# Later, split additions of exponentials, six conversion buffers, two tiles for the turned q and k, and another order at the outset and at the first norm, in an attention kernel followed by a SwiGLU FFN

## The chip, the cores and the metric

The kernel runs on one core of a Trainium2 chip. The metric is the device time of one execution in microseconds (us). Executions of one kernel agree to about 0.3%. A ratio is the mean time of one kernel's fast runs over the mean of the other's of the same rounds, so it is not quite the ratio of the medians that are quoted beside it. "Same" means within 2%.

## The reference

```python
# q, k, v: (8, 12, 448, 64) float32; g_q, g_k: (64,); w_gate, w_val: (768, 1536), w_out: (1536, 768), float64
q_n, k_n = rmsnorm(q, g_q), rmsnorm(k, g_k)            # over the 64 of each head
scores = q_n @ k_n.T / sqrt(64)
attn = exp(scores - max); attn = attn / (attn.sum(-1) + 1e-9)
x = (attn @ v), heads side by side                      # (3584, 768)
xn = x / sqrt(mean(x*x) + 1e-6) * rms_g
out = (silu(xn @ w_gate) * (xn @ w_val)) @ w_out        # (3584, 768) float32
```

There are 8 sequences with 6 pairs of heads each, so 48 pairs, numbered on through the sequences. A sequence has 448 rows: three blocks of 128 and a last one of 64, which the kernel calls "rests".

## The kernel before

The engines run in an order fixed by hand. Each `pe(fn)` is one step of TensorE (PE); `after(n, fn)` puts work for other engines n steps later in the program. The attention of later pairs is mixed with the FFN of earlier sequences. During the first 300 us the float64 weights are also turned into float32 with integer operations, in 72 pieces:

```python
NW, NH = 27, 14                                   # slots for weights
raw_pool, cv_pool = pool("c_raw", 6), pool("c_cv", 4)
...
def split(raw):                                   # ACT; raw is the loaded float64
    top = cv_pool.tile([128, BW], I32, name="top")
    nc.scalar.activation(top.bitcast(F32), hi.bitcast(F32), ACT.Abs)                   # L719
    nc.scalar.activation(lo, lo.bitcast(U32), ACT.Copy, scale=2.0**-29)                # L720
def join(lo, hi, top):                            # DVE: three instructions, L725 to L727
...
def convert():                                    # one turn, called about once per PE step
    n = turn_of["n"]
    ...
    if 0 <= n - 4 < len(pieces):                  # POOL: L763, frees top and raw
        nc.gpsimd.tensor_tensor(data(key).bitcast(I32), top, lo, ALU.add)
    if 0 <= n - 3 < len(pieces):
        st["cv", n - 3] = join(*st.pop(("cv", n - 3)))
    if 0 <= n - 2 < len(pieces):
        st["cv", n - 2] = split(st.pop(("raw", n - 2)))
    if n < len(pieces):
        st["raw", n] = load_raw(pieces[n][1])     # transfer, 384 KB, into one of six raw buffers
    if 0 <= n - 6 < len(pieces):
        keep(pieces[n - 6][0])
```

A `raw` buffer lives from its transfer to the addition in POOL (GpSimd), because `lo` and `hi` are views of it. Six raw buffers thus mean: the transfer of piece n waits for the addition of piece n-6.

The sums of exponentials, for pairs past the first seven, on POOL:

```python
def add():                                        # in score()
    rest = st["e", g, "rest"]
    for j in range(2):
        r = across(j)
        es = st["es", g, j] = tmp.tile([128, S], F32, name="es", tag="es", bufs=4)
        nc.gpsimd.tensor_tensor(es, st["e", g, 0, j], st["e", g, 1, j], ALU.add)
        nc.gpsimd.tensor_tensor(es, es, st["e", g, 2, j], ALU.add)
        nc.gpsimd.tensor_tensor(es[r], es[r], rest[r], ALU.add)
if NK - 1 in cs and not direct(g):
    after(4 if g == NPAIR + 1 else 1, add)
```

The rests of the next sequence are loaded in the third pair of a sequence and normed, on POOL, in the fourth and fifth. For sequence 2 these are pairs 9 and 10, while weights are still being converted:

```python
def rms():                                        # in norm_rests(), POOL
    nc.gpsimd.tensor_scalar(ms, ms, 1.0 / D, 1e-6, ALU.mult, ALU.add)
    nc.gpsimd.tensor_tensor(rq, ms[0:D], half[0:D], ALU.pow)
    nc.gpsimd.tensor_tensor(rest[0:D], rest[0:D], rq..., ALU.mult)
    for place in range(2):
        nc.gpsimd.tensor_tensor(st["rr", b][own(place), lo:hi], ms[own(1), :, place], half[own(1), :, place], ALU.pow)
...
def some_rests(g):
    b, hp = divmod(g, NPAIR)
    if g == 1:
        norm_rests(0, 3, NPAIR)
    elif hp in (3, 4):
        norm_rests(b + 1, 3 * (hp - 3), 3 * (hp - 2))
...
        if hp == 2:
            load_rests(b + 1, nc.sync)
            load_v_rests(b + 1)
```

The order at the first norm of x (pair 7), and the copies of the turned (transposed) q and k out of PSUM, where PE's results land:

```python
        if g == NPAIR + 1:
            pe(lambda: rms_x(0))
            pe(lambda: score(g, (1, 2)))
            pe(lambda: norm_x(0))
        pe(lambda: sums(g - 1))
...
    nc.scalar.activation(dst[:, 0, :], ps[:, 0:S], ACT.Copy, scale=gqk[:, 0:1])    # L519, q by ACT
    nc.vector.tensor_copy(dst[:, 1, LAST], ps[:, S:])                              # L520, k's last columns by DVE
```

## Time and profile before

| | before |
|---|---|
| median of 4 runs (lowest, highest) | 1641.48 us (1638.43, 1642.02) |
| span of the profiled execution | 1636.1 us |
| PE busy in that span | 1595.4 us (98%) |
| PE idle before 480 us / from 480 to 1400 us | 32 us / 1.3 us |

The time is PE's time. So the profile is read by looking for the places where PE stands still or runs at half clock (its granted clock falls to 0.5), and for what it waits for there. All of them lie before 480 us. The lines are in the prediction below. In the tables by stage the columns are: stretch and its length, then busy time and number of instructions of PE, of PE's weight loads, of DVE (VectorE), ACT (ScalarE) and POOL, then the granted clock of PE, the DMA share and GB/s.

### The profile page before, as it was taken

To read this page: it belongs to the slowest core of one execution; us is meant where nothing else is said; L and a number is where in the kernel's file an instruction comes from. 1 tells how busy PE (TensorE), PEld (TensorE's weight loads), DVE (VectorE), ACT (ScalarE), POOL (GpSimd) and SP (SyncE) were. 2 spreads that over 40 slices of the span, in tenths; PEclk is the share of its full clock that TensorE was granted. 3 is DMA by queue.
4 is the path that set the end of the run, shared out by engine and by line. 5 is a ranking of instruction groups with operands and counts; after the bars stand their busy time and mean duration, and the time that the engine had idled before them with its cause. 6 is when DMAs were issued, how large, how long until landed. Compare 5 with 4: busy or idle time off the path is not lost.

```text
span 1636.1 us, 21612 instructions
## 1 busy us (share of the span) xinstructions
PE 1595.4 (98%) x7328; PEld 1125.6 (69%) x7328; DVE 873.6 (53%) x1490; ACT 476.4 (29%) x944; POOL 672.0 (41%) x706
## 2 busy tenths in 40 slices
PE   7999899999999999999999999999999999999998
PEld 3344444577865787758885588847877587969974
DVE  4779888568872354525564245633556234433431
ACT  6755444322232223222322223222232123100110
POOL 7867786545434433433542354324534322200000
PEclk8999999999999999999999999999999999999999
DMA  7657456456665654485554655466544564557641
GB/s 188 195 163 223 156 178 197 154 190 227 226 216 154 202 156 135 124 260 148 160 151 138 175 159 155 140 189 202 160 137 118 161 179 116 150 183 237 174 143 49
DMA packets 264587, 276.81 MB, mean 169 GB/s; under 512 B 79124, under 2 KB 261396, under 8 KB 264468
## 3 DMA queue, kind: packets, MB, share of 16 engines
q1 hardware_dynamic: 262740, 274.95, 56.3%
q8 instruction: 60, 0.98, 0.3%
q10 hardware_dynamic: 1600, 0.39, 0.1%
q14 instruction: 59, 0.48, 0.1%
q0 software_dynamic: 128, 0.00, 0.0%
HBM read 235.93 MB, written 39.32 MB: 168 GB/s over the span
## 4 chain that ended last, share of the span: by engine, by line
PE 83%; DVE 9%; POOL 3%; DMA 2%; issue 1%; ACT 1%; SPq 0%; DVEq 0%; POOLq 0%; ACTq 0%
PE ff L878 38%; PE ff L1076 21%; PE av L579 6%; PE sc L532 6%; PE ff L973 3%; PE den L592 2%; PE sc L556 2%; PE ff L1107 2%; DVE rd L600 2%; PE tr L515 1%; DVE top L725 1%; DVE top L726 1%; DVE top L727 1%; DVE w L835 1%; POOL rs L495 1%
## 5 line engine op out<-in xcount | busy, mean ns | idle before, releaser
L878 PE MATMUL ff<-x,w 128*128 128x224 f32 x1770 | 360.9, 355 | 3.6 <-ACT p L911 1.9
L878 PEld LDWEIGHTS ff<-x,w 128*128 128x128 f32 x1770 | 333.5, 191 | 13.5 <-issue 6.5
L543 POOL TENSOR_TENSOR es<-e 128x448 f32<-128x448 f32 x82 | 94.0, 1146 | 543.5 <-ACT e L536 540.2
L878 PE MATMUL ff<-xs,w 128*128 128x224 f32 x1326 | 272.2, 354 | 1.9 <-DVE u L890 1.6
L878 PEld LDWEIGHTS ff<-xs,w 128*128 128x128 f32 x1326 | 248.6, 190 | 8.1 <-issue 5.2
L1076 PE MATMUL ff<-w,h 128*128 128x384 f32 x600 | 203.4, 488 | 0.0
L600 DVE RECIPROCAL rd<-rd 128x448 f32<-128x448 f32 x41 | 121.1, 2953 | 128.4 <-ACT rd L599 128.4
L536 ACT ACTIVATE e<-sc,rs 128x448 f32<-128x448 f32 x288 | 162.0, 633 | 42.4 <-PE sc L532 40.8
L1076 PEld LDWEIGHTS ff<-w,h 128*128 128x128 f32 x600 | 112.6, 190 | 78.3 <-issue 4.6
L532 PE MATMUL sc<-qkT 64*128 64x448 f32 x576 | 140.8, 583 | 7.5 <-ACT e L572 6.0
L579 PE MATMUL av<-e,vt 128*64 128x448 f32 x576 | 119.0, 548 | 0.0
L1076 PE MATMUL ff<-w,so 128*128 128x384 f32 x338 | 116.6, 488 | 2.0 <-DVE y L1037 2.0
L532 PEld LDWEIGHTS sc<-qkT 64*128 64x128 f32 x576 | 54.6, 189 | 90.5 <-issue 68.7
L495 POOL TENSOR_TENSOR rs<-ms,mhalf 128x12 f32<-128x12 f32 (+1 forms) x50 | 113.2, 2263 | 4.2
L1107 PE MATMUL ff<-x,w 128*128 128x448 f32 x288 | 114.5, 552 | 0.0
L890 DVE TENSOR_TENSOR cc<-ff,u 128x448 f32<-128x448 f32 x84 | 52.3, 623 | 88.7 <-PE ff L878 88.6
L544 POOL TENSOR_TENSOR es<-es,e 128x448 f32<-128x448 f32 x82 | 94.4, 1152 | 7.8 <-ACT e L536 1.5
L545 POOL TENSOR_TENSOR es<-es,e 64x448 f32<-64x448 f32 x82 | 94.6, 1154 | 6.4
L1076 PEld LDWEIGHTS ff<-w,so 128*128 128x128 f32 x338 | 63.3, 190 | 46.4 <-DVE y L1037 3.9
L1107 PEld LDWEIGHTS ff<-x,w 128*128 128x128 f32 x288 | 54.5, 194 | 52.9 <-issue 51.3
L579 PEld LDWEIGHTS av<-e,vt 128*64 128x64 f32 x576 | 37.2, 137 | 76.9 <-issue 73.4
L763 POOL TENSOR_TENSOR w<-top,raw 128x384 int32<-128x384 int32 x72 | 76.1, 1073 | 21.8 <-DVE top L727 6.3
(123 smaller groups left out, 1964.4 us busy)
## 6 DMA issues: line engine op xcount, KB each, us to landing
w<-kept SPq DMA_DIRECT2D x480, 192.0 KB, 3.1
w<-kept_o SPq DMA_DIRECT2D x290, 192.0 KB, 2.6
kept<-w SPq DMA_DIRECT2D x94, 192.0 KB, 3.7
top<-kept SPq DMA_DIRECT2D x72, 192.0 KB, 2.8
qk<-in_q_dram SPq DMA_DIRECT2D x48, 192.0 KB, 3.9
qk<-in_k_dram SPq DMA_DIRECT2D x96, 96.0 KB, 3.1
vt<-in_v_dram SPq DMA_DIRECT2D x48, 192.0 KB, 2.5
raw<-in_moe_w_gate_dram SPq DMA_DIRECT2D x24, 384.0 KB, 4.3
```

The costliest lines, as they stand in the source:

```text
L495: nc.gpsimd.tensor_tensor(st["rs", g][:, cols], ms, mhalf[:, cols], ALU.pow)
L532: nc.tensor.matmul(ps[:, 0:S], lhsT=qkT[r, 1, c * 128:(c + 1) * 128], rhs=qkT[r, 0, :], start=True, stop=True)
L536: nc.scalar.activation(e, ps[:, 0:S], ACT.Exp, scale=rs[:, n:n + 1])
L543: nc.gpsimd.tensor_tensor(es, st["e", g, 0, j], st["e", g, 1, j], ALU.add)
L544: nc.gpsimd.tensor_tensor(es, es, st["e", g, 2, j], ALU.add)
L545: nc.gpsimd.tensor_tensor(es[r], es[r], rest[r], ALU.add)
L579: nc.tensor.matmul(av[own(j), 0:S], lhsT=vt[:, j, c], rhs=st["e", g, c, j], start=False, stop=(c == NK - 1), skip_group_check=True)
L600: nc.vector.reciprocal(rd, rd)
L763: nc.gpsimd.tensor_tensor(data(key).bitcast(I32), top, lo, ALU.add)
L878: nc.tensor.matmul(bank[:, w * HT:(w + 1) * HT], lhsT=wt[:, c * 128:(c + 1) * 128], rhs=x[:, c, :], start=onto is None and w == c == 0, st ...
L1076: nc.tensor.matmul(ps, lhsT=a, rhs=data(("wo", b, name, c)), start=first and c == 0, stop=c == NFP - 1, skip_group_check=True)
L1107: nc.tensor.matmul(bank[w][:, 0:S], lhsT=data(key)[:, c * 128:(c + 1) * 128], rhs=st["x", 0, half][:, c, :], start=half == c == 0, stop=ha ...
```

## The change

Its intent is to take away the stops in the first 300 us: POOL's additions of exponentials are to leave gaps for the conversion, and the conversion is to run further ahead. It has five parts, which this document calls A to E.

A, the additions come later and in three parts:

```diff
-        def add():
-            rest = st["e", g, "rest"]
+        def first():
             for j in range(2):
-                r = across(j)
                 es = st["es", g, j] = tmp.tile([128, S], F32, name="es", tag="es", bufs=4)
                 nc.gpsimd.tensor_tensor(es, st["e", g, 0, j], st["e", g, 1, j], ALU.add)
-                nc.gpsimd.tensor_tensor(es, es, st["e", g, 2, j], ALU.add)
-                nc.gpsimd.tensor_tensor(es[r], es[r], rest[r], ALU.add)
+        def more(of):
+            for j in range(2):
+                r = across(j) if of == "rest" else slice(0, 128)
+                e = st["e", g, of] if of == "rest" else st["e", g, of, j]
+                es = st["es", g, j]
+                nc.gpsimd.tensor_tensor(es[r], es[r], e[r], ALU.add)
         if NK - 1 in cs and not direct(g):
-            after(4 if g == NPAIR + 1 else 1, add)
+            n = 3 if g == NPAIR + 1 else 2
+            after(n, first)
+            after(n + 2, lambda: more(2))
+            after(n + 3, lambda: more("rest"))
```

B, six conversion buffers, and two slots fewer for weights:

```diff
-    NW, NH = 27, 14
+    NW, NH = 25, 14
-    raw_pool, cv_pool = pool("c_raw", 6), pool("c_cv", 4)
+    raw_pool, cv_pool = pool("c_raw", 6), pool("c_cv", 6)
```

C, two tiles for the turned q and k (the users of the tile follow, not shown):

```diff
-            st["qkT", g] = qkT_pool.tile([128, 2, S], F32, name="qkT")
+            for part in ("qT", "kT"):
+                st[part, g] = qkT_pool.tile([128, S], F32, name=part)
```

D, the outset (cut; the second half of the rests' norm, `rms_k`, also comes one step later there, and the two multiplications that change with it, of the mean and of the gains, cost the same number of instructions):

```diff
-    load_rests(0, nc.scalar)
+    load_rests(0, 0, nc.scalar)
+    load_rests(0, 1, nc.sync)
     load_pair(1)
...
     squares(0, 0)
-    norm_rests(0, 0, 1)
     warm(9)
     pe(idle)
+    norm_rests(0, 0, 1)
...
-    squares(2, 0)
...
+            pe(lambda: score(0, (0,)))
             pe(lambda: rests(0))
+            pe(lambda: score(0, (1, 2)))
+            squares(2, 0)
             squares(2, 1)
-            pe(lambda: score(0, (0, 1, 2)))
```

E, the first norm of x after the sums:

```diff
+            pe(lambda: score(g, (1,)))
             pe(lambda: rms_x(0))
-            pe(lambda: score(g, (1, 2)))
-            pe(lambda: norm_x(0))
+            pe(lambda: score(g, (2,)))
         pe(lambda: sums(g - 1))
         if g == NPAIR + 1:
+            pe(lambda: norm_x(0))
             begin(0, 15)
```

## The prediction

> **What bounds the kernel now.** I read the page first, then the busy time of each engine by stage, then what TensorE (PE) waited for, then the same waits for the other engines, then the order of time around the longest stops. The page says that PE is the bound, and the slices say where it is not:
>
> ```profile
> PE 1595.4 (98%) x7328; PEld 1125.6 (69%) x7328; DVE 873.6 (53%) x1490; ACT 476.4 (29%) x944; POOL 672.0 (41%) x706
> ...
> PE   7999899999999999999999999999999999999998
> ```
>
> The table by stage (length, then the busy time of PE, PE's weight loads, DVE, ACT, POOL, then the granted clock):
>
> ```profile
> 0.00:20.00 20.00, 13.02 (x50) 7.89 (x50) 4.76 (x13) 9.53 (x18) 14.99 (x31) 0.83 0.98 231
> 20.00:45.00 25.00, 23.23 (x114) 8.60 (x116) 17.10 (x32) 17.15 (x35) 19.65 (x23) 0.93 0.65 164
> 45.00:107.00 62.00, 56.83 (x289) 21.72 (x286) 46.39 (x76) 41.39 (x84) 49.23 (x51) 1.00 0.64 195
> 107.00:300.00 193.00, 181.49 (x622) 88.05 (x621) 173.00 (x236) 95.26 (x194) 140.85 (x133) 0.97 0.56 172
> 300.00:480.00 180.00, 173.39 (x846) 133.21 (x845) 131.32 (x227) 46.27 (x90) 78.62 (x83) 0.99 0.67 217
> 480.00:1400.00 920.00, 918.70 (x4417) 681.06 (x4416) 421.45 (x733) 247.66 (x482) 363.30 (x374) 1.00 0.55 160
> ```
>
> From 480 to 1400 us PE is idle for 1.3 us in all, so nothing that the change does there can be worth anything. What can be won lies before 480 us: 7.0 us idle in the first stage, 1.8 in the second, 5.2 in the third, 11.5 in the fourth (the weights are converted there, and DVE is 90% and POOL 73% busy), 6.6 in the fifth: 32 us. To that comes PE work at half clock: a mean of 0.97 over 193 us is 5.8 us more clock time taken away, some 3 us of work. So even a change that took away every stop would reach about 1641 - 35 = 1606; two per cent (1608.5) is out of reach in practice.
>
> The waits say who is behind the stops (in total, times, longest):
>
> ```profile
> PE sc L532 <- ACT e L572: 6.0, 2, 5.1
> PE tr L515 <- DVE qkT L520: 4.9, 3, 2.3
> ...
> ACT top L719 <- POOL w L763: 45.4, 16, 5.9
> ...
> DVE qkT L520 <- ACT qkT L519: 84.3, 28, 8.4
> ```
>
> The longest stop of PE (5.1 us, 186 to 191 us) is made by ACT's exponential of the rests, and that one stood in ACT's queue behind the conversion's first step (L719), which waited for POOL and then for a transfer:
>
> ```profile
> 186.06 0.55 ACT L719 ACTIVATE top<-raw 128x384 f32<-128x384 f32 x1 [5.25 <-POOL w L763]
> ...
> 189.89 0.55 ACT L719 ACTIVATE top<-raw 128x384 f32<-128x384 f32 x1 [1.85 <-DMA raw<-in_moe_w_gate_dram]
> ...
> 190.78 0.61 ACT L572 ACTIVATE e<-sc,rr 128x448 f32<-128x448 f32 x1
> ```
>
> Twenty microseconds earlier DVE lost time against POOL. POOL ran the six additions of exponentials in a row, and two conversions queued behind them ran without a gap; a DVE step that takes 0.355 us at the median took 3.23:
>
> ```profile
> 165.98 1.34 POOL L545 TENSOR_TENSOR es<-es,e 64x448 f32<-64x448 f32 x1
> ...
> 166.24 3.23 DVE L725 TENSOR_SCALAR top<-top 128x384 f32<-128x384 f32 x1
> 167.28 1.96 POOL L763 TENSOR_TENSOR w<-top,raw 128x384 int32<-128x384 int32 x2
> ```
>
> The chain of waits holds four such L725 (3.17, 3.17, 2.64, 2.64 us, at 139, 166, 230 and 258 us), one in most pairs of heads of this stage.
>
> **What the Trainium skill says.** SBUF — State Buffer, "Who interferes with whom": DVE and GpSimd have one port pair in common, it is locked for a whole instruction, and a DVE tensor_scalar in its two-port mode, or a DVE instruction with two SBUF inputs, is fully blocked by a GpSimd instruction. The trace agrees: 3.23 against 0.355 us. TensorE: Matmul & The Clock Gate, "Part 1: The HAM clock gate": after an idle window of about 3.4 us PE falls to half clock. The trace agrees as far as it goes: the slice 180 to 200 us, with the 5.1 us stop, has a granted clock below 1, and so has 260 to 280 us, after stops of 0.9 and 2.3 us. The same page, "Architectural detail": ACT, DVE and GpSimd queues are strict first in, first out. That is what the exponential behind L719 shows.
>
> **The change, part by part.**
>
> Exponentials added later. Nothing is removed: per pair still six additions of 1.15 us. Before, they are issued one step after the last scores and wait there for the exponentials (L543 waits 2.4 us at 160 us), and the one conversion add that each 1.2 us step of PE (three matmuls of 0.39 us) brings queues behind 7 us of additions. After, they are issued as 2, 2 and 2 at two, four and five steps, so conversions get in between and DVE finds gaps. I expect the long L725 to lose 2 us each, in about six pairs; DVE then reaches L478 earlier, POOL its norms, the conversion adds, the raw transfers and the exponential earlier.
>
> Six conversion buffers (slots 27 to 25, six instead of four given back at the end, so 31 slots as before). The add of piece n-6 instead of n-4 frees the buffer. Of the 45.4 us ACT waits I expect two thirds gone. But the raw ring keeps six, and its transfer takes 3.7 us: the add at 186.05 was followed by a landing at 189.8 us. Six buffers alone would therefore leave the 189.89 start as it is; the two parts need each other.
>
> Of the 14.4 us in this stage (11.5 idle, 3 clock) I take 60%: **-8.5 us**. For 45 to 107 us only the buffers count: ACT waited 2.3 and 4.1 us at 63 and 76 us, and PE lost 0.25 and 1.56 us at 80 and 83 us after the second: **-1.5 us**.
>
> q and k turned in two tiles. L520 (copy of k's last columns, 0.22 us) no longer waits for L519 (ACT's copy of q), which starts from the same matmul: DVE lost 84.3 us in 28 waits, mostly where DVE had time. The bank of the transposes is held until L519 is read in any case, so the 4.9 us of PE's waits shrink by 0.2 us each. In the fifth stage DVE (73% busy) gets fewer blocked moments from it and from the spread additions. **-1 us** of 6.6.
>
> The outset. Two of the four issues of the rests go from ACT to the other queue: ACT's table load starts after 2 issues (2.1 us) instead of 4 (4.0), and its first square at about 4.0 instead of 5.47, as q has landed at 3.4. But POOL's rest norm then waits for the rests of k, which landed at 8.6 (ACT squared them at 8.76) and are issued no earlier; they are now ahead of pair 1's loads, so perhaps 0.7 us sooner. POOL's chain (norm of q, rests, k, pair 1) runs without a hole up to L518 at 20.36 us; it moves by 0.7 to 1.4 us. The other order of rr and rs of k and of scores and rests moves work that lies beside this chain. **-1.5 us.**
>
> The first norm of x goes the other way. Before:
>
> ```profile
> 103.17 1.15 PE L639 MATMUL rb<-ident,rs 112*128 112x112 f32 x8
> 104.25 2.48 PE L592 MATMUL den<-e,ones 128*64 128x448 f32 x12
> 106.65 3.65 PE L1107 MATMUL ff<-x,w 128*128 128x448 f32 x9
> ...
> 104.36 3.64 DVE L646 SCALAR_TENSOR_TENSOR x<-x,rg,rb 128x448 f32<-128x448 f32 x6 [2.62 <-PE rb L639]
> 107.91 2.95 DVE L596 RECIPROCAL rd<-den 128x448 f32<-128x448 f32 x1
> ```
>
> The six scalings ran beside the sums, and the first FFN matmul followed without a stop. After, the sums come first: den ends near 104.7, DVE takes the reciprocal (2.95) and the product (0.62) to 108.4, then three scalings of 0.61 for the first half of x to 110.2, while PE has rb done at 105.9. PE stops for some 4 us and L1107 starts 3.5 us later than before. Part of it is made up, since the conversions run on meanwhile: **+3 us**.
>
> Sum: -8.5 - 1.5 - 1 - 1.5 + 3 = **-9.5 us**, so 1641.4 - 9.5 = **1632 us**.
>
> **Rivals.** (1) The raw ring becomes the bound: with the adds no earlier, ACT still waits, now named as the raw transfer, and the fourth stage keeps 10 us of its stops. For it: 1.85 us at 189.9 and 1.3 to 1.7 us of the same wait in four other pairs. Against it: the adds themselves come earlier when POOL is free. Time: 1638. (2) The stops come from DVE's load, not from its collisions: 173 us busy of 193 leaves little, and interleaved additions collide with more DVE steps, if shorter. Time: 1638 to 1642, since the norm's 3 us remain. (3) Everything is recovered, and the half-clock windows go with it: fourth stage -13, outset -3: 1625. A loss in the long FFN stages would need es to come too late for the sums; some ten steps of PE lie between, so I leave it out.
>
> **Range and chances.** The gain's size is uncertain by about as much as itself; rival 3 and a norm that costs nothing give 1623, rivals 1 and 2 together 1642. Range 1624 to 1641. Faster by over 2% would need nearly all of the 35 us; slower by over 2% would need a stop that nothing in the profile hints at.
>
> **What would show it.** Right: L719's wait for POOL falls from 45 us to under 20; the longest L725 falls under 2 us; PE's wait on the rest exponential at 186 us falls under 2 us; DVE's L520 wait on L519 goes; a new stop of 3 to 4 us stands before the first FFN matmul near 106 us; 480 to 1400 us still takes 920 us. Wrong: if the fourth stage is as long as before, or the norm's stop does not appear, or the stage after 480 us changes.

## The result, and the profile after

| | before | after |
|---|---|---|
| median of 4 runs (lowest, highest), us | 1641.48 (1638.43, 1642.02) | 1639.15 (1638.35, 1641.94) |
| ratio, 95% interval | | 0.9993 (0.9975 to 1.001) |
| profiled span, us | 1636.1 | 1636.6 |

The time is the same. It lies inside the predicted range, but the gain of 9.5 us is not there: no difference can be told.

Three stages of the kernel after, to be held against those that the prediction shows of before:

```profile
45.00:107.00 62.00, 55.09 (x278) 20.04 (x276) 48.49 (x72) 39.81 (x80) 48.21 (x50) 0.97 0.62 186
107.00:300.00 193.00, 181.34 (x627) 88.39 (x623) 158.11 (x239) 95.10 (x196) 140.93 (x131) 0.96 0.58 177
...
480.00:1400.00 920.00, 918.70 (x4417) 681.24 (x4416) 419.69 (x735) 247.65 (x483) 364.65 (x374) 1.00 0.55 160
```

DVE is relieved as intended: 158.1 us busy between 107 and 300 us, 173.0 before. But PE is no busier there (181.3 against 181.5), and its clock is 0.96 against 0.97. From 480 us on nothing changed.

Fixed stretches hide where time moves, because the same work stands at another time in each kernel. A better ruler is the start of the same matmul in both traces. Its difference, after minus before, is called the lag here:

| where (time in the kernel before) | lag | change over the stretch | predicted for it |
|---|---|---|---|
| end of the outset, 45 us | +1.57 | +1.57 | -1.5 (outset) |
| values of pair 6, 98 us | +3.04 | +1.47 | -1.5 (buffers) |
| FFN of sequence 0 well under way, 114 us | +8.30 | +5.26 | +3 (norm) |
| second norm of x, 274 us | +3.63 | -4.67 | -8.5 (additions and buffers) |
| third norm of x, 474 us | +1.00 | -2.63 | -1 (two tiles) |
| last FFN matmul | +0.55 | -0.45 | 0 |

So a gain is there (7.3 us between 114 and 474 us), and about as much is lost before 114 us. PE's waits between 45 and 300 us in the kernel after (total, times, longest):

```profile
PE sc L535 <- ACT e L581: 7.5, 2, 4.1
PE tr L519 <- POOL qn L503: 4.3, 2, 3.0
PE ff L1116 <- DVE x L655: 3.3, 1, 3.3
```

Four stops hold most of it: 3.0 us at 85 us (1.6 before), 3.3 at 113 (none before), 4.1 at 197 (5.1 before, at 191) and 3.5 at 229 (0.9 before, at 221). ACT's waits in the same stretch:

```profile
ACT top L728 <- DMA raw<-in_moe_w_out_dram: 17.2, 4, 8.0
ACT top L728 <- DMA raw<-in_moe_w_val_dram: 11.2, 2, 5.6
ACT top L728 <- POOL w L772: 11.0, 2, 5.7
```

L728 is the split of before (L719). Its wait for POOL went from 45.4 to 11.0 us, as predicted, and a wait of 28.4 us for the raw transfers stands in its place.

The step of DVE that POOL used to block, by its line: the kernel before in the first fence, the kernel after in the second. The three times are the shortest, the median and the longest in ns:

```profile
L725 DVE TENSOR_SCALAR top<-top x72: 343/355/3237, 22.0 to 297.4; 128x384 f32<-128x384 f32 x72
```

```profile
L734 DVE TENSOR_SCALAR top<-top x72: 342/353/1172, 22.2 to 298.6; 128x384 f32<-128x384 f32 x72
```

Five of the 72 took over 2 us before, none after. That part did what it was to do.

The long stop at 197 us. POOL, then ACT, the queue of transfers and PE in the kernel after, each in order of time (start, length, engine, line, instruction):

```profile
185.69 1.63 POOL L455 TENSOR_TENSOR rq<-msr,mhalf 64x6 f32<-64x6 f32 x1
...
188.42 2.03 POOL L460 TENSOR_TENSOR rr<-msr,mhalf 64x3 f32<-64x3 f32 x2
190.53 6.17 POOL L772 TENSOR_TENSOR w<-top,raw 128x384 int32<-128x384 int32 x6
...
195.79 0.55 ACT L728 ACTIVATE top<-raw 128x384 f32<-128x384 f32 x1 [5.71 <-POOL w L772]
...
196.69 0.61 ACT L581 ACTIVATE e<-sc,rr 128x448 f32<-128x448 f32 x1
...
191.91 0.37 SPq L719 DMA_DIRECT2D raw<-in_moe_w_gate_dram  x1
...
197.35 3.35 PE L535 MATMUL sc<-qT,kT 64*128 64x448 f32 x7 [4.07 <-ACT e L581]
```

This is read from the bottom up. PE waits for the exponential of the rests (L581), which stands in ACT's queue behind a split (L728). The profile names POOL as the one that the split waited for, but the first of POOL's six additions ended at 191.89 us. The semaphore that the split waits on is that of the raw load issued at 191.91, when that addition had given its buffer back, and its last update came at 195.71; a transfer of this kind took 4.3 us at the median here, and the split started 3.9 us after the issue. The addition itself had stood behind 5.1 us of POOL work for the rests of the next sequence (L454 to L460, 185.36 to 190.45). So the chain is: norm of the rests on POOL, one addition, one transfer, split, exponential, PE. It is the same chain, with the same lengths, as in the kernel before:

```profile
182.97 1.97 POOL L458 TENSOR_TENSOR rr<-msr,mhalf 64x3 f32<-64x3 f32 x2
185.02 4.15 POOL L763 TENSOR_TENSOR w<-top,raw 128x384 int32<-128x384 int32 x4
```

There the norm ended at 184.94, the first addition and the issue of its transfer came at 186.03 and 186.06, the split at 189.89. With four conversion buffers or with six, the piece that ACT waits for is not loaded earlier, since it needs one of the six raw buffers. With six buffers six additions stood in line behind the norm instead of four. The stop at 229 us has the same form around pair 10's norm of rests; there two additions of exponentials, which A had moved back, stood right ahead of the norm.

The first norm. PE (first three lines) and DVE in the kernel after:

```profile
106.41 2.48 PE L601 MATMUL den<-e,ones 128*64 128x448 f32 x12
108.81 1.14 PE L648 MATMUL rb<-ident,rs 112*128 112x112 f32 x8
113.26 3.36 PE L1116 MATMUL ff<-x,w 128*128 128x448 f32 x5 [3.30 <-DVE x L655]
...
109.00 2.96 DVE L605 RECIPROCAL rd<-den 128x448 f32<-128x448 f32 x1 [3.28 <-PE den L601]
111.99 0.62 DVE L616 TENSOR_TENSOR x<-av,rd 128x448 f32<-128x448 f32 x1
112.53 3.63 DVE L655 SCALAR_TENSOR_TENSOR x<-x,rg,rb 128x448 f32<-128x448 f32 x6
```

As worked out in the prediction: the reciprocal, the product and the first scalings now lie one after the other between the sums and the first FFN matmul, and PE stops for 3.30 us. After it PE ran at half clock from 114.0 to 117.5 us, which cost 1.7 us more (the lag goes from 6.61 at the first FFN matmul to 8.30).

### The profile page after: what moved, and what is told of

It reads as the page before. It is cut to its first block, busy times and chain, and to the rows that moved or that the text cites. A ratio compares the mean times of both kernels' runs of the same rounds, so it can differ in the third digit from the quotient of the medians.

```text
span 1636.6 us, 21588 instructions
## 1 busy us (share of the span) xinstructions
PE 1593.6 (97%) x7328; PEld 1124.5 (69%) x7328; DVE 857.5 (52%) x1490; ACT 475.7 (29%) x944; POOL 678.3 (41%) x706
## 4 chain that ended last, share of the span: by engine, by line
PE 85%; DVE 6%; POOL 3%; DMA 2%; issue 1%; SPq 1%; ACT 1%; POOLq 0%; DVEq 0%; ACTq 0%
PE ff L887 38%; PE ff L1085 21%; PE sc L535 6%; PE av L588 6%; PE ff L982 3%; PE ff L1116 3%; PE den L601 2%; PE sc L565 2%; PE tr L519 2%; DVE rd L609 1%; POOL w L772 1%; DVE rd L605 1%; DVE w L844 1%; POOL rs L498 1%; POOL es L552 1%
## 5 line engine op out<-in xcount | busy, mean ns | idle before, releaser
L887 PE MATMUL ff<-x,w 128*128 128x224 f32 x1608 | 326.7, 353 | 3.7 <-ACT p L920 2.0
L887 PEld LDWEIGHTS ff<-x,w 128*128 128x128 f32 x1608 | 301.6, 190 | 12.7 <-issue 5.9
L887 PE MATMUL ff<-xs,w 128*128 128x224 f32 x1248 | 256.3, 353 | 0.3 <-DVE cc L899 0.2
L887 PEld LDWEIGHTS ff<-xs,w 128*128 128x128 f32 x1248 | 234.0, 190 | 5.6 <-issue 4.6
L552 POOL TENSOR_TENSOR es<-es,e 64x448 f32<-64x448 f32 (+1 forms) x164 | 193.2, 1189 | 6.3
L1085 PE MATMUL ff<-w,h 128*128 128x384 f32 x568 | 192.6, 487 | 0.0
L535 PE MATMUL sc<-qT,kT 64*128 64x448 f32 x576 | 141.2, 589 | 10.1 <-ACT e L581 7.5
L535 PEld LDWEIGHTS sc<-qT,kT 64*128 64x128 f32 x576 | 55.5, 190 | 91.5 <-issue 73.7
L1085 PE MATMUL ff<-w,so 128*128 128x384 f32 x302 | 104.6, 488 | 2.0 <-DVE y L1046 2.0
L899 DVE TENSOR_TENSOR cc<-ff,u 128x448 f32<-128x448 f32 x84 | 52.3, 623 | 87.3 <-PE ff L887 87.1
L1116 PEld LDWEIGHTS ff<-x,w 128*128 128x128 f32 x288 | 54.5, 194 | 56.2 <-issue 50.6
L887 PE MATMUL ff<-x,top 128*128 128x224 f32 x408 | 85.4, 354 | 0.0
```

The source lines that it names most:

```text
L535: nc.tensor.matmul(ps[:, 0:S], lhsT=kT[r, c * 128:(c + 1) * 128], rhs=qT[r, :], start=True, stop=True)
L552: nc.gpsimd.tensor_tensor(es[r], es[r], e[r], ALU.add)
L887: nc.tensor.matmul(bank[:, w * HT:(w + 1) * HT], lhsT=wt[:, c * 128:(c + 1) * 128], rhs=x[:, c, :], start=onto is None and w == c == 0, st ...
L899: nc.vector.tensor_tensor(add[name], ps[:, 0:S], add[other], ALU.add)
L1085: nc.tensor.matmul(ps, lhsT=a, rhs=data(("wo", b, name, c)), start=first and c == 0, stop=c == NFP - 1, skip_group_check=True)
L1116: nc.tensor.matmul(bank[w][:, 0:S], lhsT=data(key)[:, c * 128:(c + 1) * 128], rhs=st["x", 0, half][:, c, :], start=half == c == 0, stop=ha ...
```

## The experiments

All kernels below are correct, ran in five rounds beside the kernel before, and are compared with it. "Rests early" (R) is no part of the change: it is an edit made up to test the reading of the long stops.

| kernel | parts | median, us | ratio to before, 95% interval |
|---|---|---|---|
| n1_norm | A B C D | 1635.48 | 0.9969 (0.9956 to 0.9983) |
| n2_outset | A B C E | 1639.60 | 1.0002 (0.9989 to 1.0015) |
| n3_both | A B C | 1634.29 | 0.9967 (0.9954 to 0.9979) |
| n4_rests | A B C D E + R | 1630.31 | 0.9951 (0.9937 to 0.9965) |
| m1_best | A B C D + R | 1625.95 | 0.9919 (0.9904 to 0.9934) |
| m2_adds | B C D | 1642.36 | 1.0013 (1.0001 to 1.0026) |
| m3_buffers | A C D | 1632.49 | 0.9960 (0.9947 to 0.9973) |
| m4_onetile | A B D | 1634.13 | 0.9970 (0.9957 to 0.9983) |
| p1_beforerests | R | 1635.94 | 0.9979 (0.9966 to 0.9992) |
| p2_best4 | A C D + R | 1634.47 | 0.9958 (0.9943 to 0.9973) |
| p3_addsonly | A | 1632.26 | 0.9954 (0.9942 to 0.9966) |
| p4_bufonly | B | 1642.23 | 1.0012 (0.9999 to 1.0025) |
| q1_raw7 | A C D, 7 raw and 5 conversion buffers | 1632.34 | 0.9952 (0.9937 to 0.9968) |
| q2_three | A B + R | 1625.28 | 0.9918 (0.9902 to 0.9933) |
| q3_noadds | B + R | 1634.46 | 0.9965 (0.9951 to 0.9980) |
| r1_outsetonly | D | 1641.01 | 1.0001 (0.9985 to 1.0016) |
| r2_normonly | E | 1644.80 | 1.0034 (1.0020 to 1.0048) |
| r3_bestraw7 | A + R, 7 raw and 5 conversion buffers | 1632.66 | 0.9956 (0.9940 to 0.9973) |

The theory at the start was: the gain of A is real, the norm (E) and the outset (D) give it back, and the stops at 197 and 229 us are made by the norm of the rests and by the raw ring. The rival was that the stops come from the load and the collisions of DVE and POOL as a whole, so that they would move but not go.

### The norm and the outset, each taken out of the change

**n1_norm**: the change without E, so the order of before at the first norm.

```diff
-            pe(lambda: score(g, (1,)))
             pe(lambda: rms_x(0))
-            pe(lambda: score(g, (2,)))
+            pe(lambda: score(g, (1, 2)))
+            pe(lambda: norm_x(0))
         pe(lambda: sums(g - 1))
         if g == NPAIR + 1:
-            pe(lambda: norm_x(0))
             begin(0, 15)
```

> The changed kernel with one part undone: at pair 7 the scores, the first norm of x and the sums are in the order of before (norm ahead of the sums). Theory (the gain of the conversion stage was given back by the first norm, +3.6 us of stop and some 1.7 us of half clock after it, and by the outset, +1.6): the stop of 3.3 us before the first FFN matmul is gone, and the time is 3 to 5 us under the changed kernel, so about 1635. Rival (the conversion stage is paced by the conversions themselves; a later start of PE only eats into stops that would come anyway): the stop is gone, but the lag of PE at 300 us against before stays at about +3 us, and the time stays at 1638 to 1640.

The ratio fell from 0.9993 to 0.9969, some 3.9 us (the intervals just overlap; r2 below comes back to the size). The first FFN matmul followed the sums without a stop (PE in the trace of this kernel):

```profile
107.11 2.48 PE L601 MATMUL den<-e,ones 128*64 128x448 f32 x12
109.52 6.66 PE L1116 MATMUL ff<-x,w 128*128 128x448 f32 x17
```

The two long stops (3.9 us at 193 and 3.5 at 224) stayed. So E costs about 4 us inside the change, and does nothing for the long stops.

**n2_outset**: the change with the order, the queue of the rests and the place of the squares of before at the outset.

```diff
-    load_rests(0, 1, nc.sync)
+    load_rests(0, 1, nc.scalar)
...
+    norm_rests(0, 0, 1)
     warm(9)
     pe(idle)
-    norm_rests(0, 0, 1)
...
+    squares(2, 0)
...
-            pe(lambda: score(0, (0,)))
             pe(lambda: rests(0))
-            pe(lambda: score(0, (1, 2)))
-            squares(2, 0)
             squares(2, 1)
+            pe(lambda: score(0, (0, 1, 2)))
```

> The changed kernel with the outset undone: rests of k issued by ACT, rests' norm, squares of pair 2 and the first scores in the order of before. Theory: the lag of +1.6 us at 30 us is gone (it came from the reduces of pair 2 standing ahead of k's copy on DVE, and from a longer stretch at half clock), time 1 to 2 us under the changed kernel. Rival (the half clock falls by chance of its window's place, in any run): no clear difference, within 1 us.

1.0002 against 0.9993 for the whole change: the intervals overlap, so D neither gains nor costs anything that can be told. The theory missed, and the rival came true.

**n3_both**: n1 and n2 together.

> The changed kernel with both undone, so before plus the later additions, the six buffers and the two tiles. Theory: the sum of the two, 4 to 7 us under the changed kernel, 1632 to 1635, which is the conversion stage's gain laid bare. Rival: as before, 1638 to 1641, since the conversion stage is paced by the raw ring and POOL.

0.9967, the same as n1 alone. The time lies in the theory's range, but it is no sum of two gains: D is worth nothing with E out as well.

**r1_outsetonly** and **r2_normonly**: D alone and E alone on the kernel before (the diffs are those of the change).

> The kernel before with the outset of the change alone (rests of k issued by the other queue, order of the rests' norm, of pair 2's squares and of the first scores; the two tiles left out). From the changed kernel's trace: the transposes of pair 1 start 2 us earlier and then wait for POOL's rests, which are only 0.8 us earlier, and pair 2's reduces stand ahead of k's copy on DVE. Theory: same within 1.5 us of before, 1639.5 to 1642, PE 0.5 to 2 us behind before at 30 us. The prediction's term: 1.5 us faster.

1.0001. The trace shows why an earlier start gave nothing. ACT's first work, a load of its function table, started at 2.14 us instead of 4.01, and pair 1 was turned 3 us earlier, until PE came to the rests:

```profile
18.99 0.47 PE L521 MATMUL tr<-ident,rest 128*128 128x128 f32 x1 [3.19 <-POOL rest L456]
```

In the kernel before the same stop is 1.59 us, at 20.36: POOL's norm of the rests came only 1.4 us earlier (it ended at 18.94 instead of 20.30), so PE stood waiting for half of what it had won. Most of the other half went to DVE's queue, where two reductions of pair 2 (L481, 1.00 us) now stood ahead of the copy of k that the next scores needed (L525):

```profile
20.31 1.00 DVE L481 TENSOR_REDUCE ms<-sq 128x6 f32<-128x384 f32 x2
21.23 0.55 DVE L525 COPY qkT<-tr 128x384 f32<-128x384 f32 x1
```

The scores of pair 1 started at 21.92 us here and at 22.23 in the kernel before: 0.3 us were left of 3. Then PE ran at half clock (0.50 between 20 and 25 us, 0.82 in the kernel before), and at 29 us the lag was -0.09, not the 0.5 to 2 us that were expected. In the trace of the whole change the half clock lasted longer, from 18.5 to 28.7 us, and its lag there was +1.57.

> The kernel before with the first norm after the sums and nothing else. Theory (a stop of 3.3 us ahead of the first FFN matmul, and half clock after it): 1643 to 1646. Rival (before, the conversions' pace absorbs it): 1640 to 1642.

1.0034, so 5.6 us. The same stop of 3.30 us stood before the first FFN matmul. But the lag was already +3.63 us at 98 us, before any code that differs, with more half clock than the trace of before has (0.86 between 85 and 95 us and 0.83 between 95 and 105, 1.00 in both before). It went to +7.20 at the first FFN matmul and to +8.90 with the half clock after the stop. So what this trace lost is not all the norm's. Four pairs of kernels differ by E alone: it costs 5.6 us on the kernel before (r2), 3.9 in the whole change (n1), 5.7 without D (n2 to n3) and 5.2 with the rests early (n4 to m1 below). That is some 4 to 6 us, and the stop of 3.3 us with 1.7 us for the half clock after it lies within that.

### The long stops: the norm of the rests

**n4_rests**: the whole change, with the rests of sequence 2 loaded in pair 7 and normed in pairs 7 and 8, instead of 8, 9 and 10.

```diff
         if g == 1:
             norm_rests(0, 3, NPAIR)
+        elif b == 1:
+            if hp in (1, 2):
+                norm_rests(2, 3 * (hp - 1), 3 * hp)
         elif hp in (3, 4):
             norm_rests(b + 1, 3 * (hp - 3), 3 * (hp - 2))
...
-        if hp == 2:
+        if hp == 2 and b != 1 or g == NPAIR + 1:
```

> The changed kernel with one thing added: the rests of sequence 2 are loaded at pair 7 and normed at pairs 7 and 8 instead of 9 and 10. Theory for the two long stops that stayed (4.1 us at 197 us and 3.5 us at 229 us, both at the pairs in which POOL norms rests for 5.9 us with the conversions queued behind it): they go, or move to pairs 7 and 8 and are shorter there because POOL has idle time (7.5 us at 117 us); time 3 to 6 us under the changed kernel. Rival (the stops come from the raw transfers' latency of 3.7 us alone): the stops stay where they are, no difference.

0.9951 against 0.9993, about 7 us. PE's waits between 45 and 300 us:

```profile
PE ff L1116 <- DVE x L655: 3.3, 1, 3.3
...
PE sc L535 <- ACT e L581: 1.0, 1, 1.0
```

The two stops of 4.1 and 3.5 us became one of 1.0. The stop of the norm of x stayed, as it had to. So the norm of the rests in pairs 9 and 10 was what made the long stops. (Their load moves one pair earlier too; no run takes that by itself.)

**m1_best**: n4 without E.

> The first norm in the order of before and the rests of sequence 2 normed at pairs 7 and 8: both repairs together on the changed kernel. Theory (two causes that do not overlap): 1630.3 for the rests alone less the 4 us that the norm's order was worth, 1625 to 1628, the fastest so far, with no stop of PE over 3 us between 60 and 310 us. Rival (PE then only runs into the conversions' pace somewhere else): 1629 to 1631, with a new stop.

0.9919: the gains of n1 (0.0024) and n4 (0.0042) add up to 0.0066, and 0.0074 was measured. No stop of PE between 60 and 310 us was over 3 us, and between 107 and 300 us PE was busy for 188.8 us at full clock, 7.5 us more than in the kernel after:

```profile
107.00:300.00 193.00, 188.80 (x665) 92.69 (x665) 169.09 (x245) 96.01 (x198) 151.25 (x140) 1.00 0.57 180
```

**p1_beforerests**: the kernel before with the rests early, nothing of the change.

> The kernel before, with nothing of the change, and the rests of sequence 2 normed at pairs 7 and 8 instead of 9 and 10. Theory (the long stop at 186 us and the one at 220 us are made by the rests' norm on POOL ahead of the conversions, whatever the additions do): both go, which is 5.1 and 0.9 us and the half clock after the first, so 1632 to 1635. Rival (the additions in a row are needed for the stops' cause, so without their spreading POOL is as late as ever): under 2 us gained, 1638 to 1640, with a stop of 3 us or more left between 180 and 230 us.

0.9979. The stops moved to 133 us (1.1) and 164 us (2.4) and shrank, but L725 kept its long cases (3.24 us at most, six over 2 us). Alone the early rests are worth 3.4 us, half of what they are worth with the change: more than the rival allowed, less than the theory.

### The additions, the buffers and the tiles, each taken out or put in alone

**m2_adds**: n1 with the additions of before (so without A and E).

```diff
-            n = 3 if g == NPAIR + 1 else 2
-            after(n, first)
-            after(n + 2, lambda: more(2))
-            after(n + 3, lambda: more("rest"))
+            after(4 if g == NPAIR + 1 else 1, add)
```

> The changed kernel with the first norm as before (1635.5) and the additions of exponentials as before (six in a row, one step after the scores). Theory of the prediction (the spread additions free DVE from its long waits at the port and with it POOL's norms): DVE's L734 step has again its cases of 2.6 to 3.2 us, and the time is 3 to 6 us longer, 1638 to 1641. Rival (spreading moves as much work of POOL into the time just ahead of the rests' norm, 2.6 us at 215 us, as it frees): the long L734 come back, the stop at 224 us shrinks from 3.5 to about 1 us, and the time is the same within 1.5 us.

1.0013 against n1's 0.9969: 7 us are lost. The stop at 196 us was 5.6 us, and the DVE step had its long cases again (five over 2 us, 3.26 at most).

**p3_addsonly**: A alone on the kernel before (its diff is A's above).

> The kernel before with the additions in three parts and nothing else. Theory (this part alone is the change's gain, the others are nothing or a loss): 1632 to 1635, as the run with four buffers and the first norm as before (1632.5), no DVE step L725 over 1.5 us. Rival (it needs the six buffers or the two tiles): 1637 to 1640.

0.9954, 7.5 us. This one part is better than the whole change. The DVE step took 1.18 us at most, and PE's longest stops were two of 2.9 us:

```profile
PE sc L532 <- ACT e L578: 5.8, 2, 2.9
```

The trace shows where the gain lies. Stops of 0.79, 1.49, 0.94 and 2.29 us at 153, 237, 262 and 265 us in the kernel before, in which PE waited for copies by DVE or for POOL's L613, became one of 0.77 us at 263 and a new one of 0.83 at 122. The stop at the exponential of the rests fell from 5.1 to 2.9 us, but the next one grew from 0.9 to 2.9. Whether it is the later start or the three parts that does this, no run separates.

**m3_buffers**: n1 with four conversion buffers and 27 slots (so without B and E).

```diff
-    NW, NH = 25, 14
+    NW, NH = 27, 14
-    raw_pool, cv_pool = pool("c_raw", 6), pool("c_cv", 6)
+    raw_pool, cv_pool = pool("c_raw", 6), pool("c_cv", 4)
```

> The changed kernel with the first norm as before (1635.5) and four conversion buffers with 27 slots, as before. Theory (the raw ring of six with its transfer of 3.7 us after the same add is the next bound, so two more buffers only rename the wait): ACT's wait before L728 goes from raw transfers back to POOL's adds at about the same 40 us in all, and the time is the same within 1.5 us. Rival (the buffers are what the change gained): 1639 to 1641.

0.9960 against n1's 0.9969: taking the buffers away did not cost, it gained 1.5 us, though the intervals overlap. The stops were 3.0 and 2.9 us instead of 3.9 and 3.5, the stop at 84 us was 1.6 instead of 3.0, and there was no half clock at 97 us. ACT's wait was back in its old place (41.8 us for POOL). The wait of ACT was not what bound the stage.

**p4_bufonly**: B alone on the kernel before.

> The kernel before with six conversion buffers and 25 slots and nothing else. Theory (renames the wait and lets PE run into POOL at 85 us): 1640 to 1643, equal or a little slower than before, ACT's wait before L719 on raw transfers instead of POOL. Rival of the prediction (two thirds of ACT's 45 us gone and PE's stops with them): 1634 to 1638.

1.0012. The waits of ACT changed their names:

```profile
ACT top L719 <- DMA raw<-in_moe_w_val_dram: 15.7, 4, 6.0
ACT top L719 <- DMA raw<-in_moe_w_out_dram: 12.8, 4, 4.7
ACT top L719 <- DMA raw<-in_moe_w_gate_dram: 8.2, 2, 5.9
...
ACT top L719 <- POOL w L763: 6.0, 1, 6.0
```

Together they are 42.7 us; before, 45.4 us were put down to POOL. The longest stop of PE was 5.7 us (5.1 before), and at 84 us it was 2.9 (1.6 before).

**m4_onetile**: n1 with q and k in one tile (so without C and E).

```diff
-            for part in ("qT", "kT"):
-                st[part, g] = qkT_pool.tile([128, S], F32, name=part)
+            both = qkT_pool.tile([128, 2, S], F32, name="qkT")
+            for i2, part in enumerate(("qT", "kT")):
+                st[part, g] = both[:, i2, :]
```

> The changed kernel with the first norm as before (1635.5) and q's and k's turned copies in one tile again. Theory (DVE's copy of k's last columns waits for ACT's copy of q in both cases, 87.1 us in 28 waits after against 84.3 before, so the two tiles freed nothing that matters): same within 1 us, and the same 28 waits. Rival (the scores start earlier because they wait for the tiles apart): 1 to 3 us longer.

0.9970 against 0.9969. C is worth nothing. DVE's wait, in the kernel after (two tiles) and here (one tile):

```profile
DVE kT L523 <- ACT qT L522: 87.1, 28, 8.4
```

```profile
DVE qkT L524 <- ACT qkT L523: 86.2, 28, 8.4
```

It is the same 28 waits. So the tile in SBUF was not their cause.

### The raw ring, and why six buffers gave nothing

**q1_raw7**: n1 with seven raw, five conversion buffers and 24 slots, the same memory.

```diff
-    NW, NH = 25, 14
+    NW, NH = 24, 14
-    raw_pool, cv_pool = pool("c_raw", 6), pool("c_cv", 6)
+    raw_pool, cv_pool = pool("c_raw", 7), pool("c_cv", 5)
```

> The changed kernel with the first norm as before (1635.5) and seven raw buffers, paid for with one conversion buffer (five) and one slot (24). The chain at the long stops is: rests' norm ends, first add 1.0 to 1.4 us, its raw transfer 3.8 us, split, exponential. Theory (the raw ring makes it): with seven the last split ahead of the exponential needs the raw data freed one add earlier, before the norm, so the stops of 3.9 and 3.5 us shrink by 1.5 to 3 us each and the time is 1629 to 1633. Rival (POOL's adds queued behind the norm are the bound in any case): stops as long, 1634 to 1637.

0.9952 against n1's 0.9969. The stops of 3.9 and 3.5 us shrank to 0.8 and 1.5, and ACT's waits for raw transfers went from 34 us in n1 to under half a microsecond in all; what is left is named POOL again:

```profile
ACT top L728 <- POOL w L772: 31.2, 10, 7.9
```

One raw buffer more did for the stops what two conversion buffers more had not. This supports the raw ring as what held the stops in the kernel after; the 2.8 us in time are not clear of the noise, since the intervals of q1 and n1 overlap. A ring of seven beside six conversion buffers and 25 slots does not fit in the memory.

**p2_best4**: m1 with four conversion buffers and 27 slots. Since B had been worth nothing or less so far, the theory was that it would be so here too.

> The fastest so far (first norm as before, rests early, 1626.0) with four conversion buffers and 27 slots. Theory (the two more buffers let ACT run ahead and pay with a stop of 2.95 us before the transposes at 85 us, which the run with four buffers lacked, and a half-clock window after it): 1623 to 1625, no stop at 85 us. Rival (once the rests are out of the way the buffers do earn something in the conversion stage): 1627 to 1629.

The theory missed. 0.9958 against m1's 0.9919: with the rests early and the additions split, the six buffers earn some 6 us. The trace shows where. Stretches of 20 us in p2_best4, then in m1_best (the number before the last two is the granted clock):

```profile
140.00:160.00 20.00, 20.00 (x57) 9.99 (x55) 18.08 (x28) 10.12 (x21) 15.01 (x15) 0.92 0.61 197
160.00:180.00 20.00, 17.64 (x60) 7.34 (x59) 12.65 (x18) 10.19 (x21) 14.43 (x15) 0.91 0.71 227
```

```profile
140.00:160.00 20.00, 20.00 (x75) 9.32 (x73) 19.13 (x33) 9.00 (x20) 17.86 (x17) 1.00 0.64 207
160.00:180.00 20.00, 19.05 (x60) 9.75 (x57) 16.72 (x21) 13.90 (x30) 18.11 (x18) 1.00 0.73 236
```

With four buffers PE stopped for 2.7 us at 138.5 and 2.4 us at 169, and after each stop its clock fell to half for a while: 57 matmuls instead of 75 between 140 and 160 us. With six the longest stops between 100 and 250 us were 1.0 us at 161 and 1.6 us at 192, and the clock stayed full. The same matmuls lay 1.1 us earlier at 128 us, 6.2 at 147 and 9.2 at 178; some of it was given back later, and 8 us remained at 474 us.

**q2_three**: A, B and the early rests on the kernel before, without C, D and E.

> The kernel before with three things: additions in three parts, six conversion buffers, rests of sequence 2 at pairs 7 and 8. Theory (two tiles and outset are worth nothing): as the fastest so far, 1624.5 to 1628. Rival (they are worth something once the stops are gone): 1629 or more.

0.9918, 1625.28 us: the fastest kernel, level with m1, so C and D are worth nothing in this company either.

**q3_noadds**: q2 without A.

> The kernel before with six conversion buffers and the rests of sequence 2 at pairs 7 and 8, additions as before. Theory (the spread additions free DVE and POOL in any arrangement, worth 7 to 8 us): 1632 to 1636, with DVE's L725 of 2.6 us or more. Rival (with the rests moved POOL has room and the additions in a row no longer hurt): 1625 to 1629.

0.9965. The DVE step had four cases over 2 us again, and a stop of 2.6 us stood at 192 us. So A is worth 7.7 us here (0.9965 to 0.9918).

**r3_bestraw7**: q2 with seven raw, five conversion buffers and 24 slots.

> Additions in three parts and rests early on the kernel before (as the fastest, 1625.3), with seven raw buffers, five conversion buffers and 24 slots instead of six, six and 25. Theory: with the rests moved no long stop is left for the longer ring to shrink: same within 2 us, 1623.5 to 1627.5. Rival: PE gains another 2 to 4 us in the conversion stage: 1621 to 1623.

0.9956, some 6 us slower than q2: theory and rival both missed. Stops of 1.4 us stood at 137 and 165 us. Of the 8.6 us that this kernel's matmuls lay behind q2's at 461 us, 2.3 had come by 340 us and the rest after, with stretches of half clock at 358 and 461 us. By then the conversion is over and its buffers serve as slots, so this kernel has 29 slots (24 and five) where q2 has 31 (25 and six). That is the likely reason: q1, with 29 too, has the same stops of 3.0 us at 358 and 2.0 at 459 us, where n1, m3 and q2 with 31 have 2.0 and 0.3. No run takes it by itself. Once the rests are early, six and six is the better share of the memory.

The eight combinations of additions split, buffers and early rests then stand as follows (ratio to before, where two kernels have the same three parts and differ in C or D, both):

| | four conversion buffers | six |
|---|---|---|
| additions as before | 1, 1.0001 | 1.0012, 1.0013 |
| additions split | 0.9954, 0.9960 | 0.9967, 0.9969, 0.9970 |
| rests early, additions as before | 0.9979 | 0.9965 |
| rests early, additions split | 0.9958 | 0.9918, 0.9919 |

Without the early rests six buffers cost some 2 us in either row (1.1 to 2.6, by which kernels are paired). With them they earn 2 us, and 6 us where the additions are split. Only these 6 us are clear of the noise: the interval of p4 reaches 0.9999, that of m2 1.0001, and those of p1 and q3 overlap, as do those in the row of the split additions. With the rests early the additions alone are worth 3.4 us (p1 to p2) and the buffers alone 2.3 (p1 to q3), neither clear of the noise, but both 10 (p1 to q2): there the two parts do need each other, as the prediction had said.

## Why the prediction was right or wrong

**Additions split: right, in the mechanism at DVE and about right in size.** The long cases of the DVE step went (3.24 us at most before, 1.17 after), by A alone (p3) and not without A (m2, q3). A alone is worth 7.5 us, nearly the 8.5 that the prediction gave to the fourth stage for A and B together. The stop at 186 us that it was to end is still 2.9 us with A alone and 4.1 in the change; the gain came at PE's stops for DVE instead.

**Six buffers: this is the step that failed most.** The prediction said that six buffers alone leave the start of the late split as it is because the raw ring keeps six, that "the two parts need each other", and then booked a common gain of 8.5 us and 1.5 more for the buffers between 45 and 107 us. The two parts did not help each other. In the traces the split waited for the raw transfer instead of for POOL (28.4 us, and 45.4 became 11.0), the transfer could start only when POOL, behind its norm of the rests, gave a raw buffer back, and up to six additions stood in line there in place of four. Measured, A and B together give 5 us (5.4 in n3, 4.9 in m4) where 10 were booked, and B takes some 2 us of what A gives alone. Between 45 and 98 us nothing was won: the stop before pair 6's transposes grew from 1.6 to 3.0 us in all kernels with six conversion buffers (PE came to it earlier and POOL's norm of q no sooner), so the lag across it stayed at +1.2 to +1.5. The further +1.6 came with a stretch of half clock at 97 us, which r1 and p3 show too, without the six buffers, and m3 and the kernel before do not. It is not the buffers' doing: the same stop of 1.98 us stands ahead of it in all of these, and the clock falls or not by where the stop lies on a grid of 3.41 us (see the last section). Rival 1 of the prediction (the raw ring becomes the bound, 1638 us) is what happened: q1 shows it by one more raw buffer, n4 by taking the norm out of POOL's way. The missing piece was that POOL's norm of the rests heads this chain. The prediction had the line of the split that waited, and looked for its cause in the additions 20 us earlier, not in what POOL had done in the 5 us before.

**The first norm: right in mechanism, its size too small.** The stop is 3.30 us and the first FFN matmul moved by 3.57 us (lag 3.04 to 6.61), where 3.5 was predicted. "Part of it is made up" did not come true: half clock followed instead, and the lag rose to 8.30. Taken out, it gives 3.9 to 5.7 us in four pairs; predicted were 3.

**Outset: wrong.** -1.5 us was expected, 0 measured (n2, n3, r1). The prediction had seen that POOL's norm of the rests sets the time, and that it would move by 0.7 to 1.4 us; it did move (1.4 us in r1). It had not seen that the two reductions of pair 2 would move ahead of the copy of k in DVE's queue and take that back.

**Two tiles: wrong.** -1 us was expected, 0 measured (m4). The prediction took the wait of DVE's copy on ACT's copy for a matter of the SBUF tile. It stayed with two tiles. PE's own stops for this copy did shrink (3.8 us between 45 and 300 us before, 0.8 after), but by A: they are 1.6 us with A alone (p3) and 3.9 with B alone (p4). Both copies read the same PSUM tile, `ps`, and the Trainium skill says of that (PSUM — Partial Sum Buffer, "PSUM bank collisions raise a hardware error") that two engines which access the same bank and quadrant at once collide, ScalarE and VectorE reading included, and that they have to be kept apart by semaphores. Had the prediction looked there it might have dropped this term. That the bank is the cause fits m4 and the traces; no run here gave the last columns a bank of their own. The 2.6 us that the lag fell between 274 and 474 us are not from the tiles: 1.6 of them are a stretch of half clock at 368 us in the trace of before that after lacks.

**After 480 us: right.** 918.70 us busy of 920 in both.

**The signs and a sum.** Of the signs that it named, ACT's wait for POOL under 20 us (11.0), the long DVE step under 2 us (1.17), the stop before the first FFN matmul (3.3) and the unchanged long stage came; the stop at the rests' exponential under 2 us (4.1) and the end of DVE's wait for ACT's copy (87.1) did not. And its 3 us for the half clock in the fourth stage are too few: its own trace holds 10.2 us of half clock there (190.5 to 197.3 and 265.6 to 269.0 us), which costs nearly 5 us of work.

**The sum.** Taken singly, A is -7.5 us, B +2, C 0, D 0, and E +4 to +6. That makes some -1.5 to +0.5; the change measured 0.9993, or -1.1 us. So the gain did come, and was given back by two of the other parts.

## What to carry to other kernels

When an engine waits in a chain of buffer rings, adding buffers to one ring changes the name of the wait before it changes the time: ask which ring the next transfer needs, and what the engine that frees it is doing just then. Test the parts of a bundle singly and in pairs; here one part alone (1632.3 us) beat the bundle of five (1639.2), and a part that cost 2 us in it earned 6 us once a norm of 5 us had been moved out of the way (1625.3 us). Count a stop of two to three microseconds on PE with the half clock that may follow it, some 1.7 us more.

## What the Trainium skill lacked or had wrong

- TensorE: Matmul & The Clock Gate, "Why this matters for your kernels", advises against idle gaps over about 3 us, and "What's actually happening" speaks of a whole idle window of about 3.4 us. Here shorter stops were followed by half clock: 2.69 us at 138.5 and 2.36 us at 169 in p2_best4 (clock 0.92 and 0.91 in the 20 us slices), 3.30 us at 113 in the kernel after, and already 2.29 us at 265 in the kernel before, which the prediction counted as agreement. Stops of 1.0 and 1.6 us in m1_best were not. But length alone does not decide: in m1_best a stop of 2.95 us at 85 us was not followed by it, and one of 1.98 at 97 was. In each trace the stretches of half clock start whole steps of 3.41 us apart (at 97.0, 114.0, 196.0 and 230.1 us in the kernel after). Cut along these steps, the 20 traces (40 to 1600 us) show 75 steps at full clock that were followed by one at half clock, and PE stood still for 1.5 us or more in each of them. All 43 steps with 2.0 us or more were followed by half clock; of the steps followed by full clock none had more than 1.98. The stop of 2.95 us fell across a border (1.54 and 1.40 us). So a given stop may or may not cost the 1.7 us, by where it falls.
- SBUF — State Buffer, "Who interferes with whom", says that the loser of the port pair is blocked for a whole instruction. It does not say that a row of GpSimd instructions without a gap can keep it out for longer: a DVE step of 0.355 us took 3.23 us across three of them, and at most 1.18 us once the additions came in pairs.
- No page gives a duration for a power on GpSimd. Here 64x6 elements took 1.63 us, two of 64x3 together 2.03 us, and these few numbers headed the chain behind PE's longest stop.
